# Program order for the evacuations of a seven-product matrix product, and four stores moved to one queue

## Chip, cores and metric

The kernel runs on one core of a Trainium2 chip. The metric is device microseconds of one execution, as the median of several runs. Beside the times there is one profiled execution, from which all rows below come.

## What is computed

Attention with a window of 128 and eight heads over 4 sequences of 576, then an MLP with ELU, then an MLP with leaky ReLU. The change lies in the second MLP and at the end of the first.

```python
x = np.ascontiguousarray(attn_out.transpose(0, 2, 1, 3)).reshape(B * S, H * D)   # 2304 x 512
# first MLP: d_ff 2048
h = x @ w_in
g = np.where(h > 0.0, h, 1.0 * (np.exp(np.minimum(h, 0.0)) - 1.0))
x = g @ w_out
# second MLP: d_ff 2048
h = x @ w_in
g = np.maximum(0.01 * h, h)
out = g @ w_out
```

## The kernel before

All matrix products run on operands that are split into a high and a low float32r part, so that one product is three matmuls (high by high, high by low, low by high; `split_mm`, L303). The split is always the same pair: a copy to float32r on ScalarE (the high part) and a subtraction on VectorE (the low part).

**First MLP.** Attention and the first MLP are interleaved over five blocks of tokens (`BLK1`). For each block, 16 chunks of the hidden width pass through `mlp1_h` (L559) and `mlp1_y` (L595). When the last chunk of a block is done, its result lies in four banks y0 to y3. They are copied to tiles ys, the even ones by ScalarE, the odd ones by VectorE (L619 to L622), and each is stored to x2T in DRAM (L625). The stores of the first three blocks are issued by SyncE, those of the last two by GpSimd (odd) and ScalarE (even).

**Second MLP, first product.** It works on three groups of 768 tokens (`GRP`) and, inside a group, on eight pairs of 128-wide chunks of the hidden width: 24 units. A unit multiplies a 2 x 2 block matrix of weights with a 2 x 2 block matrix of tokens by seven block products in place of eight (Strassen-Winograd). Each product is six matmuls of 128x128 by 128x384 (`product`, L820). The weight operands (tiles h1, h2 with their low parts) are sums of weight blocks, made earlier and kept in DRAM; they are loaded to a tile s for each pair (`s_load`, L742) and split for each unit (`split_w`, L748). The token operands (tiles x2) are sums of the four token blocks of a group. The group is loaded from x2T to a tile xr (`x2_load`, L765), and `x2_job` (L770) makes the seven operands in seven jobs, each a split and up to two subtractions.

`unit(u)` (L843) writes the work in this order: product 1 into bank x and copy s1 of it by ScalarE (L850); product 5 into bank z; product 4 of the unit before and its activation c21 (L856); product 6 into x and copy a by VectorE (L860); product 3 of the unit before, sum c12 on VectorE (L864) and its activation; product 2 into bank w, sum c11 (L869) and activation; product 7 into x, copy b by ScalarE (L873), sum c22 on VectorE (L875) and activation. Products 6, 7 and 4 go on adding to the bank that was copied just before, so each waits for that copy: 6 for s1, 7 for a, 4 (in the next unit) for b. In the profile the banks x, z, w are px, pz, pw. `g2_out` (L831) does the activation (L833, ScalarE) and the store to g2T in DRAM: by GpSimd for groups 0 and 1, by SyncE for group 2 (L836). The tiles a and c21 share three slots; a slot of c21 comes free when its store has landed.

**Second MLP, second product.** It reads g2T back and has the same seven products in another order (`second`, L936).

**What sets the order.** Matmuls are kept in the order of the program (`matmul`, L135). The other engines' instructions are placed by a scheduler, which takes them where it expects their operands and slots to be ready. Calls through the wrappers `act`, `dve`, `pool` are also kept in program order while `Ordered.on` is set (L126 to L131). Before the change the first product's evacuations and splits are called on `nc.scalar` and `nc.vector`, and so left to the scheduler. Each engine runs its instructions strictly in the order that results.

Of the kernel before, what the change touches and what calls it, by code (L numbers as in the profile page):

```python
# [10 lines left out]
F32 = mybir.dt.float32  # L11
# [4 lines left out]
AF = mybir.ActivationFunctionType  # L16
ALU = mybir.AluOpType
# [13 lines left out]
BLK1 = [(0, 512), (512, 256), (768, 512), (1280, 512), (1792, 512)]  # L31
# [67 lines left out]
def attention_elu_leaky_kernel(  # L99
# [13 lines left out]
    nc = tc.nc  # L113
# [481 lines left out]
    def mlp1_y(J, cs, gg):  # L595
        gh, gl = gg
        t0, n = BLK1[J]
        per = 512 // n
        if cs[0] == 0:
            Y[J] = [psp.tile([P, per, n], F32, tag=f"y{i}", name=f"y{i}") for i in range(NK // per)]  # L600
        for ci, i, m in [(ci, i, m) for ci in range(len(cs)) for i in range(3) for m in range(NK)]:
            woh, wol = weights(1, cs[ci], 1)
            w, g = ((woh, gh), (woh, gl), (wol, gh))[i]

            matmul(Y[J][m // per][:, m % per, :], w[:, m * P:(m + 1) * P], g[:, ci * n:ci * n + n],
                             start=cs[ci] == 0 and i == 0 and m % per == 0, stop=cs[ci] == NC - 1 and i == 2,
                             skip_group_check=True)
        if cs[-1] == NC - 1:
            if J == len(BLK1) - 1:

                all_ys = wp.tile([P, NK, n], F32, tag="w15", name="ys")
            for i, y in enumerate(Y.pop(J)):
                if J == len(BLK1) - 1:
                    ys = all_ys[:, i * per:i * per + per]
                elif J == len(BLK1) - 2 and i > 1:
                    ys = l2.tile([P, per, n], F32, tag="ex", name="ys", bufs=2)
                else:
                    ys = egp.tile([P, per, n], F32, tag="eg", name="ys")
                if i % 2:  # L619
                    nc.vector.tensor_copy(ys, y)  # L620
                else:
                    nc.scalar.copy(ys, y)  # L622

                q = nc.sync if J < len(BLK1) - 2 else nc.gpsimd if i % 2 else nc.scalar
                q.dma_start(out=x2T[:, i * per:i * per + per, t0:t0 + n], in_=ys)  # L625


# [142 lines left out]
    def x2_job(g, n):  # L770

        xr = Xr[g]

        def b(j, k):
            return xr[:, 2 * j:2 * j + 2, k * HALF:(k + 1) * HALF]

        def sub(o, x, y):
            nc.vector.tensor_tensor(o, x, y, op=ALU.subtract)

        def split(name, src):  # L780
            i = OPERANDS.index(name)
            home = OP_HOMES[g][i]
            if home == "x1":
                two = g, i // 3
                if two not in OP:
                    OP[two] = x1p.tile([P, 2, 2, 2, HALF], F32R, tag="x1", name="x2")
                t = OP[two][:, i % 3 % 2]
            else:
                t = (l2 if home[0] == "a" else wp).tile([P, 2, 2, HALF], F32R, tag=home, name="x2")
            nc.scalar.copy(t[:, 0], src)  # L790
            nc.vector.tensor_tensor(t[:, 1], src, t[:, 0].bitcast(F32), op=ALU.subtract)
            OP[g, name] = t[:, 0], t[:, 1]

        if n == 0:
            split("b11", b(0, 0))
            sub(b(0, 0), b(0, 1), b(0, 0))
            sub(b(0, 1), b(1, 1), b(0, 1))
        elif n == 1:
            split("t1", b(0, 0))
            sub(b(0, 0), b(1, 1), b(0, 0))  # L800
        elif n == 2:
            split("t2", b(0, 0))
            sub(b(0, 0), b(1, 0), b(0, 0))
        elif n == 3:
            split("b21", b(1, 0))
        elif n == 4:
            split("t3", b(0, 1))
        elif n == 5:
            split("t4", b(0, 0))
        elif n == 6:  # L810
            split("b22", b(1, 1))

    ps2, first, queue = {}, [], []

    def feed(n=1):
# [14 lines left out]

    def g2_out(u, c, half, tile_, src):  # L831
        g, p = divmod(u, NP2)
        nc.scalar.activation(tile_, src, AF.Prelu, alpha=0.01)  # L833
        t0 = g * GRP + half * HALF
        last = g == NG - 1
        store = (nc.sync if last else nc.gpsimd).dma_start(out=g2T[:, 2 * p + c, t0:t0 + HALF], in_=tile_)  # L836
        if last:
            tc.keep_in_program_order(store)
# [4 lines left out]
    def unit(u):  # L843

        if u < NU:
            x, z, w = (psp.tile([P, HALF], F32, tag=tg[u % 2], name=nm)
                       for tg, nm in ((("s0", "s1"), "px"), (("h", "c"), "pz"), (("y0", "y1"), "pw")))
            product(1, u, x, True)
            s1 = small(glp, "gh", "s1")
            nc.scalar.copy(s1, x)  # L850
            product(5, u, z, True)
        if u:
            x_, z_, a_ = ps2.pop(u - 1)
            product(4, u - 1, x_, False)
            c21 = small(glp, "gl", "c21")
            g2_out(u - 1, 1, 0, c21, x_)  # L856
        if u < NU:
            product(6, u, x, False)
            a = small(glp, "gl", "a")
            nc.vector.tensor_copy(a, x)  # L860
        if u:
            product(3, u - 1, z_, False)
            c12 = small(egp, "eg", "c12")
            nc.vector.tensor_tensor(c12, z_, a_, op=ALU.add)  # L864
            g2_out(u - 1, 0, 1, c12, c12)
        if u < NU:
            product(2, u, w, True)
            c11 = small(egp, "eg", "c11")
            nc.vector.tensor_tensor(c11, w, s1, op=ALU.add)  # L869
            g2_out(u, 0, 0, c11, c11)  # L870
            product(7, u, x, False)
            b = small(glp, "gh", "b")
            nc.scalar.copy(b, x)  # L873
            c22 = l2.tile([P, HALF], F32, tag="ex", name="c22", bufs=2)
            nc.vector.tensor_tensor(c22, z, b, op=ALU.add)  # L875
            g2_out(u, 1, 1, c22, c22)
            ps2[u] = x, z, a

# [32 lines left out]
    def prepare(n):  # L911

        g, at_ = divmod(n, len(SEQ))
        if g == NG:
            return
        m, q = SEQ[at_]
        cell = {r: RAW4[g, r][q] for r in ("b11", "b12", "b21", "b22") if len(RAW4.get((g, r), ())) > q}
        hi, lo = CELLS[n % 5]
        role = {1: "b11", 5: "b11", 6: "b11", 4: "b11", 7: "b12", 2: "b21", 3: "b22"}[m]
        split2(hi, lo, cell[role])  # L920
        D2[n] = hi, lo

        def sub(o, x, y):
            dve.tensor_tensor(cell[o], cell[x], cell[y], op=ALU.subtract)

        if m == 1:
            sub("b11", "b12", "b11")
        elif m == 5:
            sub("b11", "b22", "b11")
        elif m == 6:  # L930
            sub("b11", "b21", "b11")
            sub("b12", "b22", "b12")
# [81 lines left out]
    def raw_cells(role, home, tag, n):  # L1014
        cells = quarters(home.tile([P, 2 * n, HALF], F32, tag=tag, name="raw"), n)
        for cell in cells:
            raw_load(0, role, len(RAW4.get((0, role), ())), cell)

    for u in range(NU):
        g, p = divmod(u, NP2)  # L1020
        unit(u)
        if 0 < u < NU - 1:
            split_w(u + 1, 1)
        if u < NU - 1:
            split_w(u + 1, 2)
        if g == 0 and p < 5:
            s_load(p + 3)
        if g and p == 0:
            x2_job(g, 5)
            x2_job(g, 6)  # L1030
        if g + 1 < NG:
            if p == (g > 0):
                x2_load(g + 1)
            elif 4 <= p <= 6:
                x2_job(g + 1, p - 4)
            elif p == 7:
                x2_job(g + 1, 3)
                x2_job(g + 1, 4)
            continue
        if p == 1:  # L1040
            raw_cells("b11", l2, "xr", 4)
            xa = quarters(x1p.tile([P, 10, HALF], F32R, tag="x1", name="cells"), 5)
            CELLS += [(xa[0], xa[1]), (xa[2], xa[3])]
        elif p == 2:
            hl_load(1)
        elif p == 3:
            raw_cells("b12", wp, "w15", 2)
            raw_cells("b12", wrawp, "wraw", 2)
        elif p == 4:
            hl_load(5)  # L1050
        elif p == 5:
            prepare(0)
            hl_load(6)
        elif p == 6:
            prepare(1)
# [3 lines left out]
    xb = quarters(x1p.tile([P, 10, HALF], F32R, tag="x1", name="cells"), 5)  # L1059
    CELLS += [(xb[0], xb[1]), (xb[2], xb[3]), (xa[4], xb[4])]  # L1060
    prepare(2)
    unit(NU)
    raw_cells("b22", l2, "at0", 2)
    raw_cells("b21", l2, "at1", 2)
    for _ in range(2):
# [68 lines left out]
```

## Time and profile before

| | |
|---|---|
| median of 3 runs | 893.24 us (892.77 to 893.8) |
| profiled execution, its own time | 892.43 us |
| its span | 890.7 us |
| TensorE busy | 874.3 us, 98% |
| VectorE, ScalarE, GpSimd busy | 70%, 56%, 17% |
| mean granted clock of TensorE | 0.996 |

Times in the rows are microseconds from the start of the span. PE is TensorE's matmuls, PEld its weight loads, DVE is VectorE, ACT ScalarE, POOL GpSimd and SP SyncE; a q behind a name is the engine's sequencer, which issues DMAs. L127 and L136 are the lines of the wrappers, so that operations called through them are told apart by their tiles. The granted clock is 1.00 for 2.4 GHz and 0.50 for 1.2 GHz.

### The profile page before, as it was taken

How to read it: one execution, taken by the hardware profiler on the slowest of the kernel's cores; microseconds unless marked ns; L12 is line 12 of the kernel's file. 1: busy time of each engine (PE TensorE's matmuls, PEld its weight loads, DVE VectorE, ACT ScalarE, POOL GpSimd, SP SyncE). 2: the span in 40 equal slices, each digit the busy share in tenths (PEclk: the TensorE clock that was granted, in tenths of full speed). 3: DMA queues.
4: the chain of work that ended last, by engine and by line, in shares of the span. 5: the costliest groups of instructions: out<-in, count | busy, mean ns of one | idle time of the engine just before them, and what ended most of it. 6: DMA issues, size and time to landing. Idle time of an engine off the chain costs nothing. (4 is left out here: it accounts for less than half of the span.)

```text
span 890.7 us, 14687 instructions
## 1 busy us (share of the span) xinstructions
PE 874.3 (98%) x5077; PEld 770.7 (87%) x5077; DVE 621.9 (70%) x1330; ACT 499.5 (56%) x1067; POOL 155.4 (17%) x349
## 2 busy tenths in 40 slices
PE   8999999999999999999999989999999999999998
PEld 5578878998787787878888878999999999999998
DVE  6799866556776766677554786678577695875953
ACT  7888864445455555445443645677677544444442
POOL 5802222332213211121000001322310000000000
PEclk9999999999999999999999998999999999999999
DMA  8941323221745547353599999243239899437002
GB/s 327 347 177 61 120 74 107 59 71 49 261 154 202 191 160 271 132 220 146 180 344 367 312 308 395 108 158 133 110 110 312 331 358 372 162 100 233 23 1 71
DMA packets 94746, 169.66 MB, mean 190 GB/s; under 512 B 8144, under 2 KB 63696, under 8 KB 94672
## 3 DMA queue, kind: packets, MB, share of 16 engines
q1 hardware_dynamic: 89680, 154.04, 49.9%
q0 software_dynamic: 4416, 13.64, 4.1%
q10 hardware_dynamic: 576, 1.05, 0.3%
q8 instruction: 40, 0.66, 0.3%
q14 instruction: 34, 0.28, 0.1%
HBM read 106.82 MB, written 61.87 MB: 189 GB/s over the span
## 5 line engine op out<-in xcount | busy, mean ns | idle before, releaser
L136 PE MATMUL h_ps<-x,w 128*128 128x512 f32 (+1 forms) x960 | 215.0, 373 | 0.9 <-ACT x L127 0.5
L136 PEld LDWEIGHTS h_ps<-x,w 128*128 128x128 f32 x960 | 166.1, 188 | 38.8 <-ACT x L127 4.0
L136 PE MATMUL y<-gh,w 128*128 128x512 f32 (+1 forms) x640 | 157.2, 368 | 0.0
L136 PEld LDWEIGHTS y<-gh,w 128*128 128x128 f32 x640 | 113.8, 189 | 20.0
L880 ACT CAST cells<-raw 128x768 fp32r<-128x768 f32 x84 | 70.2, 837 | 86.8 <-PE px L136 46.3
L881 DVE TENSOR_TENSOR cells<-raw,cells 128x768 fp32r<-128x768 f32 x84 | 79.5, 956 | 41.9 <-ACT cells L880 41.4
L136 PE MATMUL px<-x,h 128*128 128x384 f32 x432 | 99.8, 338 | 5.3 <-ACT s L850 2.7
L136 PE MATMUL px<-cells,a 128*128 128x384 f32 x576 | 102.1, 334 | 0.3 <-ACT c L979 0.3
L136 PEld LDWEIGHTS px<-cells,a 128*128 128x128 f32 x576 | 100.0, 188 | 0.6 <-ACT c L979 0.6
L589 ACT CAST gh<-eg 128x512 fp32r<-128x512 f32 (+1 forms) x80 | 46.2, 577 | 82.0 <-DVE eg L588 81.7
L127 POOL TENSOR_SCALAR t<-t,stat 128x128 f32<-128x128 f32 (+3 forms) x160 | 71.7, 461 | 91.0 <-DVE stat L127 86.5
L127 ACT ACTIVATE t<-t,stat 128x128 f32<-128x128 f32 (+2 forms) x160 | 62.5, 393 | 43.6 <-DVE t L127 30.1
L136 PEld LDWEIGHTS px<-x,h 128*128 128x128 f32 x432 | 77.4, 189 | 6.8 <-ACT b L873 3.3
L127 POOL TENSOR_SCALAR_AFFINE_SELECT pt<-pt 128x256 f32<-128x256 f32 (+1 forms) x112 | 45.5, 415 | 213.9 <-ACT pt L489 210.3
L136 PE MATMUL y<-gl,w 128*128 128x512 f32 (+1 forms) x320 | 78.7, 368 | 0.0
L590 DVE TENSOR_TENSOR gl<-eg,gh 128x512 fp32r<-128x512 f32 (+1 forms) x80 | 51.1, 639 | 25.4 <-ACT gh L589 25.3
L136 PEld LDWEIGHTS y<-gl,w 128*128 128x128 f32 x320 | 56.9, 189 | 10.0
L762 ACT CAST h<-s 128x512 fp32r<-128x512 f32 (+1 forms) x72 | 49.4, 692 | 27.1 <-PE pz L136 25.6
L586 ACT ACTIVATE eg<-h_ps 128x512 f32<-128x512 f32 (+1 forms) x80 | 43.9, 548 | 35.6 <-PE h_ps L136 34.2
L127 DVE CUSTOM_DVE_ANT_0 t<-s_ps,bias 128x256 f32<-128x256 f32 (+4 forms) x160 | 51.6, 370 | 3.7 <-PE s_ps L136 2.9
L136 PE MATMUL pz<-x,h 128*128 128x384 f32 x240 | 54.1, 339 | 0.0
L588 DVE TENSOR_TENSOR eg<-h_ps,eg 128x512 f32<-128x512 f32 (+1 forms) x80 | 50.8, 636 | 2.0
(83 smaller groups left out, 1347.7 us busy)
## 6 DMA issues: line engine op xcount, KB each, us to landing
raw<-g2T SPq DMA_DIRECT2D x48, 384.0 KB, 4.8
wraw<-in_w_in SPq DMA_DIRECT2D x32, 512.0 KB, 5.1
wraw<-in_w_out SPq DMA_DIRECT2D x32, 512.0 KB, 4.9
hlT<-hl SPq DMA_DIRECT2D x16, 1024.0 KB, 5.9
a<-hlT SPq DMA_DIRECT2D x56, 256.0 KB, 5.2
g2T<-c POOLq DMA_DIRECT2D x64, 192.0 KB, 2.2
four<-s_out SPq DMA_DIRECT2D x16, 512.0 KB, 7.1
g2T<-c SPq DMA_DIRECT2D x32, 192.0 KB, 3.9
```

Source lines behind the costliest of these rows:

```text
L127: ins = f(*args, **kw)
L136: tc.keep_in_program_order(nc.tensor.matmul(*args, **kw))
L586: nc.scalar.activation(g[:, :m], ps, AF.Exp)
L588: nc.vector.tensor_tensor(g[:, :m], ps, g[:, :m], op=ALU.max)
L589: nc.scalar.copy(hi[:, :m], g[:, :m])
L590: nc.vector.tensor_tensor(lo[:, :m], g[:, :m], hi[:, :m].bitcast(F32), op=ALU.subtract)
L762: nc.scalar.copy(hi[:, a:b], s[:, a + o:b + o])
L880: nc.scalar.copy(hi, src)
L881: nc.vector.tensor_tensor(lo, src, hi.bitcast(F32), op=ALU.subtract)
```

## The change

The stores of the last block of the first MLP are all issued by GpSimd. In the first product of the second MLP the copies, sums and activations of `unit` and the splits and subtractions of `x2_job` are called through `act` and `dve`; `unit` and the jobs that follow units run with `Ordered.on`. (The jobs of group 0 run during the first MLP with it off.)

```diff
-                q = nc.sync if J < len(BLK1) - 2 else nc.gpsimd if i % 2 else nc.scalar
+                q = nc.sync if J < len(BLK1) - 2 else nc.gpsimd if i % 2 or J == len(BLK1) - 1 else nc.scalar
                 q.dma_start(out=x2T[:, i * per:i * per + per, t0:t0 + n], in_=ys)
...
         def sub(o, x, y):
-            nc.vector.tensor_tensor(o, x, y, op=ALU.subtract)
+            dve.tensor_tensor(o, x, y, op=ALU.subtract)
...
-            nc.scalar.copy(t[:, 0], src)
-            nc.vector.tensor_tensor(t[:, 1], src, t[:, 0].bitcast(F32), op=ALU.subtract)
+            act.copy(t[:, 0], src)
+            dve.tensor_tensor(t[:, 1], src, t[:, 0].bitcast(F32), op=ALU.subtract)
...
+    def ordered_job(g, *ns):
+        Ordered.on = True
+        for n in ns:
+            x2_job(g, n)
+        Ordered.on = False
...
-        nc.scalar.activation(tile_, src, AF.Prelu, alpha=0.01)
+        act.activation(tile_, src, AF.Prelu, alpha=0.01)
...
-            nc.scalar.copy(s1, x)
+            act.copy(s1, x)
...
-            nc.vector.tensor_copy(a, x)
+            dve.tensor_copy(a, x)
...
-            nc.vector.tensor_tensor(c12, z_, a_, op=ALU.add)
+            dve.tensor_tensor(c12, z_, a_, op=ALU.add)
...
-            nc.vector.tensor_tensor(c11, w, s1, op=ALU.add)
+            dve.tensor_tensor(c11, w, s1, op=ALU.add)
...
-            nc.scalar.copy(b, x)
+            act.copy(b, x)
...
-            nc.vector.tensor_tensor(c22, z, b, op=ALU.add)
+            dve.tensor_tensor(c22, z, b, op=ALU.add)
...
     for u in range(NU):
         g, p = divmod(u, NP2)
+        Ordered.on = True
         unit(u)
+        Ordered.on = False
...
         if g and p == 0:
-            x2_job(g, 5)
-            x2_job(g, 6)
+            ordered_job(g, 5, 6)
         if g + 1 < NG:
             if p == (g > 0):
                 x2_load(g + 1)
             elif 4 <= p <= 6:
-                x2_job(g + 1, p - 4)
+                ordered_job(g + 1, p - 4)
             elif p == 7:
-                x2_job(g + 1, 3)
-                x2_job(g + 1, 4)
+                ordered_job(g + 1, 3, 4)
...
+    Ordered.on = True
     unit(NU)
+    Ordered.on = False
```

In the rows of the order below, a number behind a tile is the tile's own, and the brackets name the engines and DMA lanes that the instruction waits for.

The first place is ScalarE from the end of the first MLP into unit 1 of the first product, before the change. h_5778 is a weight operand of unit 2, x_6028 the first token operand of group 1; c_5687 and c_5699 are c11 and c22 of unit 0, c_5735 and c_5752 its c21 and c12, and c_5762 is c11 of unit 1.

```order
L622 COPY ys<-y_5043 128x512 [waits PE_49]
L622 COPY ys<-y_5045 128x512
L625 DMA x2T<-ys 128x512 [waits Activation_49] x2
L850 COPY s_5665<-px 128x384 [waits PE_49]
...
L850 COPY s_5721<-px 128x384 [waits PE_49]
L833 ACTIVATE c_5735<-px 128x384 [waits PE_49]
L790 CAST x_6028<-xr 128x768 [waits DMAHW3_49]
L762 CAST h_5784<-s 128x512 [waits PE_49]
L833 ACTIVATE c_5752<-c_5752 128x384 [waits DVE_49]
L762 CAST h_5857<-s 128x512 [waits DMAHW1_49,PE_49]
L833 ACTIVATE c_5762<-c_5762 128x384 [waits DVE_49]
L873 COPY b<-px 128x384 [waits PE_49,Activation_49]
```

The same place on ScalarE after the change.

```order
L622 COPY ys<-y_5043 128x512 [waits PE_49]
L622 COPY ys<-y_5045 128x512
L127 COPY s_5665<-px 128x384 [waits PE_49]
...
L127 COPY s_5721<-px 128x384 [waits PE_49]
L127 ACTIVATE c_5735<-px 128x384 [waits PE_49]
L762 CAST h_5784<-s 128x512 [waits PE_49]
L127 ACTIVATE c_5752<-c_5752 128x384 [waits DVE_49]
L127 ACTIVATE c_5762<-c_5762 128x384 [waits DVE_49]
L127 COPY b<-px 128x384 [waits PE_49,Activation_49]
L762 CAST h_5857<-s 128x512 [waits DMAHW7_49]
```

The two DMA issues behind the ys copies are gone. The token operand x_6028, which waits for a load, and the weight cast h_5857, which waits for another, no longer stand ahead of copy b of unit 1; h_5857 stands behind it, and x_6028 between c21 and c12 of the unit before, in unit 4.

The second place is GpSimd's queue from the stores of the last two blocks on, before the change.

```order
L625 DMA x2T<-ys 128x512 [waits DVE_49] x2
L836 DMA g2T<-c_5687 128x384 [waits Activation_49]
L836 DMA g2T<-c_5699 128x384 [waits Activation_49]
L836 DMA g2T<-c_5735 128x384 [waits Activation_49]
L836 DMA g2T<-c_5752 128x384 [waits Activation_49]
```

And after it.

```order
L625 DMA x2T<-ys 128x512 [waits Activation_49]
L625 DMA x2T<-ys 128x512 [waits DVE_49]
L625 DMA x2T<-ys 128x512 [waits Activation_49]
L625 DMA x2T<-ys 128x512 [waits DVE_49]
L842 DMA g2T<-c_5687 128x384 [waits Activation_49]
L842 DMA g2T<-c_5699 128x384 [waits Activation_49]
L842 DMA g2T<-c_5735 128x384 [waits DMASW0_49,Activation_49]
L842 DMA g2T<-c_5752 128x384 [waits DMASW1_49,Activation_49]
```

Four stores of 256 KB in place of two now stand ahead of the first stores of the first product.

The third place is VectorE in units 1 and 2 after the change; the first row is copy a of unit 1, c_5774 is c22 of unit 1, and the last row is copy a of unit 2.

```order
L127 COPY a<-px 128x384 [waits PE_49]
L127 TENSOR_TENSOR c_5752<-pz,a 128x384 [waits DVE_49,PE_49]
L763 TENSOR_TENSOR h_5784<-s,h_5784 128x512 [waits Activation_49]
L127 TENSOR_TENSOR c_5762<-pw,s_5721 128x384 [waits PE_49]
L127 TENSOR_TENSOR c_5774<-pz,b 128x384 [waits DMASW1_49,Activation_49]
L763 TENSOR_TENSOR l_5858<-s,h_5857 128x512 [waits DMAHW7_49,PE_49,Activation_49]
L763 TENSOR_TENSOR l_5858<-s,h_5857 128x768 [waits DMAHW4_49,Activation_49]
L127 COPY a<-px 128x384 [waits DMASW0_49,PE_49]
```

Copy a of unit 2 waits for lane DMASW0, the lane of the store of c_5735, which is c21 of unit 0. Before the change two subtractions and a split of group 1's token operands stood between these rows; they now come in units 4 and 5.

## Rows read from the trace of the kernel before

**Rows 1.** The page, busy us (share of the span) and instructions of each engine.
```profile
PE 874.3 (98%) x5077; PEld 770.7 (87%) x5077; DVE 621.9 (70%) x1330; ACT 499.5 (56%) x1067; POOL 155.4 (17%) x349
```

**Rows 2.** Busy us by stretches, PE, PEld, DVE, ACT, POOL, clock, DMA share, GB/s.
```profile
520.00:540.00 20.00, 17.26 (x81) 15.74 (x80) 12.96 (x18) 10.13 (x17) 2.16 (x4) 0.91 0.97 331
540.00:560.00 20.00, 17.97 (x95) 17.65 (x94) 13.90 (x21) 11.53 (x22) 4.61 (x9) 0.91 0.87 346
600.00:700.00 100.00, 100.00 (x577) 99.57 (x576) 72.39 (x112) 68.98 (x134) 17.11 (x32) 1.00 0.53 190
720.00:740.00 20.00, 20.00 (x117) 20.00 (x116) 17.20 (x21) 8.70 (x11) 0.00 (x0) 1.00 1.02 371
```

**Rows 3.** Line of time, TensorE, 526 to 556: start, us, operation [idle before <- releaser].
```profile
531.93 0.61 PE L136 MATMUL px<-x,h 128*128 128x384 f32 x2 [2.74 <-ACT s L850]
...
536.75 0.52 PE L136 MATMUL px<-x,h 128*128 128x384 f32 x2
...
544.04 0.51 PE L136 MATMUL px<-x,h 128*128 128x384 f32 x2
...
548.32 1.77 PE L136 MATMUL px<-x,h 128*128 128x384 f32 x8 [2.03 <-ACT b L873]
...
555.19 0.51 PE L136 MATMUL px<-x,h 128*128 128x384 f32 x2
```

**Rows 4.** Busy us by stretches, the granted clock third from the end.
```profile
532.70:536.00 3.30, 3.30 (x12) 3.30 (x11) 0.88 (x2) 0.00 (x0) 0.00 (x0) 0.50 0.99 299
...
549.80:553.10 3.30, 3.30 (x12) 3.30 (x12) 3.15 (x5) 1.14 (x3) 1.08 (x2) 0.50 1.03 408
...
225.50:229.00 3.50, 3.50 (x20) 2.67 (x18) 2.98 (x13) 1.19 (x7) 1.57 (x4) 1.00 0.97 370
```

**Rows 5.** Line of time, ScalarE and its sequencer, 529 to 549.
```profile
529.14 1.06 ACT L622 COPY ys<-y 128x512 f32<-128x512 f32 x2
529.75 1.61 ACTq L625 DMA_DIRECT2D x2T<-ys  x2
531.40 0.48 ACT L850 COPY s<-px 128x384 f32<-128x384 f32 x1 [1.19 <-issue]
...
540.08 0.49 ACT L833 ACTIVATE c<-px 128x384 f32<-128x384 f32 x1 [0.61 <-PE px L136]
545.05 0.84 ACT L790 CAST x<-xr 128x768 fp32r<-128x768 f32 x1 [4.47 <-DMA xr<-x2T]
...
547.80 0.46 ACT L873 COPY b<-px 128x384 f32<-128x384 f32 x1
```

**Rows 6.** Line of time, GpSimd, 530 to 542.
```profile
530.95 1.14 POOL L625 DMA_DIRECT2D x2T<-ys  x2 [82.89 <-DVE ys L620]
...
540.87 0.54 POOL L836 DMA_DIRECT2D g2T<-c  x1 [0.93 <-ACT c L833]
```

**Rows 7.** Line of time, TensorE, 215 to 230, in the first MLP.
```profile
224.01 1.09 PE L136 MATMUL av_ps<-pt,vr 128*64 128x128 f32 x16 [1.47 <-DVE eg L588]
```

**Rows 8.** DMA issues, 529 to 534.5: count, KB each, us to landing.
```profile
xr<-x2T SPq DMA_DIRECT2D x1, 1536.0 KB, 13.8
```

**Rows 9.** The page, costliest groups: busy us, mean ns of one.
```profile
L881 DVE TENSOR_TENSOR cells<-raw,cells 128x768 fp32r<-128x768 f32 x84 | 79.5, 956 | 41.9 <-ACT cells L880 41.4
```

**Rows 10.** Line of time of SyncE's sequencer; DMA issues around 534.
```profile
532.39 2.82 SPq L745 DMA_DIRECT2D s<-s_in  x2
...
s<-s_in SPq DMA_DIRECT2D x1, 512.0 KB, 13.7
```

**Rows 11.** DMA, 540.5 to 546.5: queue, packets, MB, share; an issue, us to landing.
```profile
q0 software_dynamic: 193, 0.59, 24.3%
...
g2T<-c POOLq DMA_DIRECT2D x1, 192.0 KB, 5.4
```

**Rows 12.** DMA queues, 534.5 to 537.5: q10 is ScalarE's, q0 GpSimd's.
```profile
q10 hardware_dynamic: 280, 0.52, 45.2%
...
q0 software_dynamic: 63, 0.25, 20.0%
```

## Prediction

> **What bounds the kernel now.** I read the page's busy times first: TensorE is busy 98% of the span [rows 1], so only TensorE's own time counts, and a change of order on the other engines can give back no more than what TensorE loses to waits and to a lower clock. Next the busy times by stretches: everywhere in the second MLP TensorE's column equals the stretch (100.00 of 100 at 600 to 700, all of 20 at 720 to 740 in the second product), except in 520 to 540 and 540 to 560, where 17.26 and 17.97 of 20 are busy and the granted clock is 0.91 [rows 2]. So the place to look is the start of the first product. TensorE's own line of time there shows two holes [rows 3]: it stands still for 2.74 us before it starts again at 531.93, and for 2.03 us before 548.32; the brackets name what ended the wait. The first hole is ended by the ScalarE copy s of bank px, the second by the copy b of the same kind. After each hole the granted clock is at 0.50, the lower of its two levels (1.2 against 2.4 GHz), for the 3.3 us that I cut out behind it [rows 4]. Last, ScalarE's line of time says why the copies were late [rows 5].
>
> **Terms used.** A unit has seven products of six matmuls. At the full clock one unit takes 544.04 - 536.75 = 7.29 us [rows 3], so a product takes 1.04 us. In a unit: products 1 and 5, then 4 of the unit before, 6, 3 of the unit before, 2, 7. Copy s must end before product 6 starts, which is two products after product 1; copy b of a unit before the next unit's product 4, two products after that unit's product 7.
>
> **The stores of the last block (ScalarE's half).** After its two ys copies ScalarE issues two stores, 1.61 us in all, and only then starts copy s, at 531.40 [rows 5]. The second issue could not start before the second ys copy was done (529.14 + 1.06 = 530.20). With the issues on GpSimd's queue copy s follows the ys copies directly: the copies of a pair overlap a little (two of about 0.58 in 1.06), so it starts at about 530.13 in place of 531.40, 1.27 us earlier; TensorE then starts at 530.66 in place of 531.93. Everything ahead of it on ScalarE stays as it was, so a hole of 2.74 - 1.27 = 1.47 us remains. **Gain 1.27.** GpSimd was idle; it gets two issues more. Its two stores of before take 1.14 us from 530.95 [rows 6], so four go from about 530.0 to 532.7, and the next thing on it (the store of c11 of unit 0) is due only after 534. The issue is hidden there; what the transfers may cost is rival B and C.
>
> **The clock after the first hole.** From product 6 of unit 0 to product 1 of unit 1 TensorE took 536.75 - 531.93 = 4.82 us for three products [rows 3]; at the full clock they take 3.12. Whether the clock falls after a hole of 1.47 us the two holes here (2.74 and 2.03) do not tell. The nearest row is the wait of 1.47 us at 224.01 [rows 7]: the stretch behind it stands at 1.00 [rows 4]. I take that row, since it has the same length: **gain 1.70**, with 0 as the other end.
>
> **Evacuations and token operands in program order.** On ScalarE the copy x (first half of the token operand b11 of group 1) stood before copy b of unit 1, and it waited 4.47 us for the load of xr [rows 5], which took 13.8 us from its issue [rows 8]. Behind it stood two weight casts, two activations, and b, which came at 547.80 while its bank was ready at about 544.1. In the new order that copy x stands in unit 4, some 15 us after the load has landed at 545.05, and no instruction ahead of b of unit 1 waits for a transfer. Product 4 then follows product 5 without a hole: at 544.04 + 2.08 = 546.12 in place of 548.32, **gain 2.20**; and products 4, 6, 3, 2, 7 take 5.20 in place of 555.19 - 548.32 = 6.87 [rows 3] at the full clock, **gain 1.67**. VectorE loses the same wait. The eleven subtractions of a group's token operands go mostly two at a time between c11 and c22 of units 4 to 8 (and 12 to 16) in place of scattered. One of this shape takes 0.96 us [rows 9], so c22 comes up to 1.9 us later; but its bank is only needed by product 3 of the next unit, four products (4.2 us) after product 7. In 600 to 700, where this work lies, VectorE was busy 72% and ScalarE 69% [rows 2], so I cost the move at 0 there; if it did not fit, a copy a would come late, at most by one such subtraction in each of ten units.
>
> **Casts that may be late next.** The weight cast for unit 4 stands ahead of copy s of unit 3, and waits for a load s. That load is the second of two issues between 532.39 and 535.21 and took 13.7 us [rows 10], so it landed by 548.9 at the latest. By the new times the cast is wanted behind copy b of unit 2, at 533.78 + 2 x 7.29 + 0.6 = 549.0 (533.78 is the new start of product 1 of unit 1), and copy s could be 1 us later without harm. The casts for units 3 and 5 have more room. I cost them at 0, and at 1 us at the upper end.
>
> **Sum.** 1.27 + 1.70 + 2.20 + 1.67 = 6.84 us, from the profiled execution's 892.43 us (span 890.7) to 885.6. The median of the runs shown is 893.24, so the forecast for the median is 893.24 - 6.84 = **886.4 us**; alone its range is 885.4 to 887.4. Behind the units the rest moves up as it is: loads and stores of the second product are issued in the order of the units, on the same queue.
>
> **Rivals.**
> A. *The clock falls after the first hole all the same.* For it: 1.47 us is not far from 2.03, after which it fell. Against it: the hole of 1.47 us without a fall. It would leave out the 1.70: 888.1. The Trainium skill (TensorE: Matmul & The Clock Gate, What's actually happening) says that the activity is watched in free-running windows, so that one kernel can meet them at another phase from run to run; by that rule a borderline hole would go either way, and the sum would be 886.4 in some runs and 888.1 in others. No run here shows such a change.
>
> B. *Stores land late and a slot is waited for.* All four stores of the last block now go ahead of the stores of c11, c22, c21 of unit 0 on GpSimd's one queue. The copy a of unit 2 takes the slot of c21 of unit 0. By the new times c21 is issued at about 537.9 (3.0 earlier than the 540.87 of [rows 6]), and with the 5.4 us of [rows 11] it lands at 543.3; copy a is wanted when product 6 of unit 2 ends, at 533.78 + 7.29 + 4.16 = 545.2, and delays product 7, two products later, only if it starts after about 546.8. Bounds: ScalarE's queue moved 0.52 MB in 3 us, 173 GB/s [rows 12]; at that rate and from 535 on, where ScalarE's stores began to move, the four stores (1.05 MB) are through at 541.1 and three small ones (0.59 MB) at 544.5. GpSimd's queue in 540.5 to 546.5 moved 0.59 MB in 6 us, 98 GB/s [rows 11]; at 98 for the small ones alone they are through at 547.1, 0.3 us too late. I take a delay of 0.3 to 1.5 us here, up to 3 with a fall of the clock: 887 to 889.5. Against it: the 98 GB/s were three small stores that came one after another, not a full queue.
>
> C. *Slower than before by the same queue.* If GpSimd's queue moves only 80 GB/s from 535 on, 1.64 MB take 20.5 us, c21 lands at 555.5, 8.7 us too late, and the clock falls once more (1.7): 886.4 + 10.4 = 896.8. The point from which it decides is 98 GB/s over the whole of it: landing at 551.7, 4.9 late, plus 1.7, which eats the whole gain. For it: the DMA engines are at their full share there, and ScalarE's queue no longer carries a part. Against it: 173 GB/s in the same crowd. The Trainium skill (DMA: Bandwidth & Descriptors, Queues, rings and completion order) has each DMA engine go round between the queues that have work. By that rule GpSimd's queue gets about half beside SyncE's, C cannot come, and the time is that of the forecast. The quarter that [rows 11] shows does not prove it, so C keeps a chance.
>
> D. *The gain does not reach the end.* In 720 to 740 the DMA engines are at 1.02 of their share [rows 2]; if the loads of the second product were held by something that does not move with the units, TensorE would wait there for what it gained, and the time would be 893. Against it: their issues follow the units, and TensorE is busy 20.00 of 20 in that very stretch [rows 2].
>
> **Chances.** Forecast 0.64, A 0.14, B 0.08, D 0.07, C 0.07. A change under 0.2% (1.8 us) cannot be told from none here. Forecast, A and B are faster by more than that: 0.86. D is the same: 0.07. C is slower: 0.07. The range takes in the forecast's own range, A and B with a fall of the clock, and leaves out C and D; A and B together stand at its upper end: 885.0 to 890.6.
>
> **What would show it.** Right: ScalarE goes from the ys copies to copy s without an issue between; one hole of about 1.5 us before product 6 of unit 0 and the clock at 1.00 behind it; no hole before product 4 of unit 1; units at 7.29 us from there on; copy x of group 1 in unit 4 with no wait for xr. Wrong: a granted clock of 0.5 after 530 (A); a TensorE hole before product 7 of unit 2 that is ended by a VectorE copy a, which itself was ended by a store of c (B, C); TensorE waits behind 704 that were not there (D).

## The result and the profile after

The changed kernel took **886.34 us** (median of 5 runs, 884.8 to 889.25) against 893.8 us for the kernel before (5 runs, 892.77 to 895.13): a ratio of 0.992, 95% interval 0.9897 to 0.9942, so 5.2 to 9.2 us less. 886.4 was forecast. The execution that was profiled is the longest of the five: 889.25 us, span 887.5.

The page of the changed kernel, engines' busy times (before: [rows 1]):

```profile
PE 872.8 (98%) x5077; PEld 769.5 (87%) x5077; DVE 623.0 (70%) x1330; ACT 498.7 (56%) x1067; POOL 157.1 (18%) x351
```

Only POOL has two instructions more, the two stores. The work is the same, so the gain is in waits and in the clock. Busy times of the changed kernel by stretches, columns as in [rows 2]; the last two stretches are 3.2 us that begin 1.5 us after TensorE's restart behind the first hole, and the place where [rows 4] has the clock behind the second:

```profile
520.00:540.00 20.00, 16.98 (x78) 15.26 (x77) 13.52 (x20) 9.95 (x16) 2.69 (x5) 0.91 0.92 299
540.00:560.00 20.00, 20.00 (x117) 20.00 (x116) 12.23 (x20) 11.64 (x24) 5.77 (x11) 1.00 1.03 412
...
720.00:740.00 20.00, 20.00 (x118) 20.00 (x117) 15.84 (x19) 7.59 (x10) 0.00 (x0) 1.00 1.05 387
534.90:538.10 3.20, 3.20 (x11) 3.20 (x11) 0.95 (x2) 0.52 (x1) 0.56 (x2) 0.50 0.99 259
549.80:553.10 3.30, 3.30 (x21) 3.30 (x21) 2.28 (x4) 1.46 (x3) 0.97 (x2) 1.00 1.04 416
```

540 to 560 was 17.97 busy at a clock of 0.91 and is now full at 1.00. In 520 to 540 nothing is better: 16.98 busy, 0.91. TensorE's line of time shows the same at single matmuls (before: [rows 3]):

```profile
533.38 0.62 PE L136 MATMUL px<-x,h 128*128 128x384 f32 x2 [3.02 <-ACT s L127]
...
538.14 0.56 PE L136 MATMUL px<-x,h 128*128 128x384 f32 x2
...
545.47 0.51 PE L136 MATMUL px<-x,h 128*128 128x384 f32 x2
...
547.55 1.55 PE L136 MATMUL px<-x,h 128*128 128x384 f32 x8
...
552.75 0.51 PE L136 MATMUL px<-x,h 128*128 128x384 f32 x2
```

The second hole is gone: product 4 of unit 1 starts at 547.55, which is 545.47 + 2.08, two products behind product 1 of unit 2, and no bracket stands there. The first hole is 3.02 us, longer than the 2.74 of before, and 4.76 us pass from its end to product 1 of unit 1 (before 4.82; 3.12 would be the full clock). ScalarE's line of time of the changed kernel (before: [rows 5]):

```profile
529.01 1.05 ACT L299 CAST hl<-four 128x1024 fp32r<-128x1024 f32 x1 [2.87 <-DMA four<-s_out]
529.97 0.82 ACT L127 CAST x<-xr 128x768 fp32r<-128x768 f32 x1
531.36 0.62 ACT L762 CAST h<-s 128x512 fp32r<-128x512 f32 x1 [0.56 <-DVE hl L300]
531.88 1.07 ACT L622 COPY ys<-y 128x512 f32<-128x512 f32 x2
532.84 0.49 ACT L127 COPY s<-px 128x384 f32<-128x384 f32 x1
...
545.44 0.53 ACT L127 ACTIVATE c<-c 128x384 f32<-128x384 f32 x1 [0.73 <-DVE c L127]
545.87 0.46 ACT L127 COPY b<-px 128x384 f32<-128x384 f32 x1
...
565.95 0.84 ACT L127 CAST x<-xr 128x768 fp32r<-128x768 f32 x1
```

VectorE's has copy a of unit 2, which follows its bank and not a store:

```profile
549.83 0.56 DVE L127 COPY a<-px 128x384 f32<-128x384 f32 x1 [0.45 <-PE px L136]
```

Copy s follows the ys copies without an issue between, as forecast, and copy b of unit 1 comes at 545.87 without copy x ahead of it; copy x stands at 565.95, without a wait. What is new to the argument is the first of ScalarE's rows. It is the cast of the last tile `four` (the load of an operand of the second product), five instructions ahead of copy s; it waits for its load, and all behind it wait with it. The weight cast two rows further waits 0.56 us more, for VectorE's subtraction of the same tile. The cast's row of the kernel before, which the prediction does not use:

```profile
526.28 1.05 ACT L299 CAST hl<-four 128x1024 fp32r<-128x1024 f32 x1 [1.80 <-DMA four<-s_out]
```

The DMA issues say in part why it starts later after (issue to landing, first the changed kernel, then the one before):

```profile
four<-s_out SPq DMA_DIRECT2D x1, 512.0 KB, 8.1
```

```profile
four<-s_out SPq DMA_DIRECT2D x1, 512.0 KB, 7.1
```

SyncE's sequencer has the rest, in the same order:

```profile
520.90 0.66 SPq L291 DMA_DIRECT2D four<-s_out  x1
```

```profile
519.18 0.66 SPq L291 DMA_DIRECT2D four<-s_out  x1
```

The load takes 1.0 us longer, and against the end of product 5 of unit 0 (530.36 after, 529.19 before) it is issued 0.55 us later: 9.46 us ahead of it in place of 10.01. In both profiles its issue comes 0.64 us behind that of the store of the split before, which goes out when VectorE has done the subtraction of that split; so a late landing one tile earlier moves this issue too.

**The first hole in one sum.** From the start of this cast to TensorE's restart it is 533.38 - 529.01 = 4.37 us after, and 531.93 - 526.28 = 5.65 us before. The difference, 1.28, is the two issues. But the cast starts 1.35 us before product 5 of unit 0 ends (533.38 - 3.02 = 530.36) after, and 2.91 us before its end (531.93 - 2.74 = 529.19) in the profile of before. So the hole is 4.37 - 1.35 = 3.02 after, against 5.65 - 2.91 = 2.74.

**Where the profiled execution's time went.** At the end of product 5 of unit 0 it was 1.17 us later than the one before (530.36 - 529.19), a difference out of the first MLP. The first hole took 0.28 more, the three products behind it 0.06 less. Then the two units with the place of the second hole: from product 1 of unit 1 to product 1 of unit 3 it is 552.75 - 538.14 = 14.61 us after, twice 7.3, and 555.19 - 536.75 = 18.44 before [rows 3]: **3.83 less**, where the prediction has 2.20 + 1.67 = 3.87. That leaves 2.44 us won at this point; the span won 3.2, and the 0.8 in the 330 us behind it I did not follow.

### The profile page after: what moved, and what is told of

The parts are those of the page before. It is cut to its first block, busy times and chain, and to the rows that moved or that the text cites. A ratio compares the mean times of both kernels' runs of the same rounds, so it can differ in the third digit from the quotient of the medians.

```text
span 887.5 us, 14689 instructions
## 1 busy us (share of the span) xinstructions
PE 872.8 (98%) x5077; PEld 769.5 (87%) x5077; DVE 623.0 (70%) x1330; ACT 498.7 (56%) x1067; POOL 157.1 (18%) x351
```

## Experiments

The theory after these rows: the moved copy x gives the second hole with its clock; the stores give 1.27 us, and the clock behind the first hole only where the load of the last `four` lands early. Rivals: the order of the units themselves is what counts; or the first hole is the stores' and should have closed. The first four kernels ran on one chip (before there: 893.98, 17 runs, 891.18 to 895.53).

**Stores alone.** The kernel before with the edit of line 624, nothing else.

> Only the stores of the last block go to GpSimd; evacuations and operands are placed as before. My theory (two separate holes): the first hole shrinks by 1.27 us, and where the clock then stays up, 1.70 us more; the second hole and its clock loss (2.20 + 1.67) stay. Time 1.3 to 3.0 us under the kernel before, about 891. Rival (the first hole is set by the late load of four that ScalarE's last cast hl waits for, not by the two DMA issues): the hole stays at 2.5 to 3 us and the time is within 0.7 us of the kernel before.

892.91 us (11 runs), ratio 0.9991 (0.9981 to 1.0001): 1.1 us less by the medians. Both holes are there:

```profile
PE px L136 <- ACT s L850: 3.0, 1, 3.0
PE px L136 <- ACT b L873: 2.9, 2, 2.3
```

This is TensorE's list of waits from 525 to 885 (us in total, times, longest); a second wait for b, 0.6 us in the last unit, is in the 2.9. ScalarE's line of time, then TensorE's:

```profile
527.87 1.05 ACT L299 CAST hl<-four 128x1024 fp32r<-128x1024 f32 x1 [2.74 <-DMA four<-s_out]
```

```profile
532.24 0.93 PE L136 MATMUL px<-x,h 128*128 128x384 f32 x2 [3.02 <-ACT s L850]
```

The hole did not shrink; it stands at 3.02, as the rival in the expectation has it. Yet from cast to restart it is 4.37 us, as in the changed kernel: the issues are gone, and the cast comes later. The gain in time fits the 1.27, but its interval (-0.1 to 1.7 us) takes in no gain too; it is too small for 1.27 and the 1.70 of a clock that stays up.

**Order alone.** The changed kernel with line 624 as it was.

> Only the program order of evacuations and token operands; the stores stay on ScalarE and GpSimd. My theory: the second hole and its clock loss go (2.20 + 1.67 = 3.9 us), the first hole stays at 2.7 us or more, with the clock at 0.50 behind it. Time about 3.9 us under the kernel before, about 889.9. Rival (the gain needs both parts, because the late store issues also hold the second hole's load): under 2 us.

888.98 us (6 runs), ratio 0.9943 (0.9924 to 0.9961), 3.5 to 6.8 us less. The second hole is gone; the first is 3.56 us, and the 5.8 us that I cut out behind it have a granted clock of 0.50. ScalarE's line of time with the order alone:

```profile
526.53 1.05 ACT L299 CAST hl<-four 128x1024 fp32r<-128x1024 f32 x1 [2.63 <-DMA four<-s_out]
...
530.01 1.59 ACTq L625 DMA_DIRECT2D x2T<-ys  x2
531.65 0.48 ACT L127 COPY s<-px 128x384 f32<-128x384 f32 x1 [1.18 <-issue]
```

TensorE's, in the same kernel:

```profile
532.18 1.01 PE L136 MATMUL px<-x,h 128*128 128x384 f32 x2 [3.56 <-ACT s L127]
```

And the stretch behind it, columns as in [rows 2]:

```profile
532.20:538.00 5.80, 5.80 (x18) 5.80 (x19) 1.12 (x2) 0.52 (x1) 0.25 (x2) 0.50 1.01 328
```

With the issues back, cast to restart is 532.18 - 526.53 = 5.65 us, as before.

**The change once more.**

> The changed kernel once more, for a second profile and five more times. If the first hole's length changes from run to run with the landing of the last load of four, runs with a mean clock of 1.000 lie 2 to 4 us under runs with 0.997 or 0.998, and this profile has another hole than 3.02 us. Rival (the hole is always 3 us and the spread comes from elsewhere): a hole of 3.0 us and a clock of 0.50 behind it again.

887.43 us (6 runs, 884.08 to 890.91), ratio 0.9922 (0.9901 to 0.9943). The profiled execution has a hole of 3.55 us; ScalarE's line of time, then TensorE's:

```profile
529.86 1.05 ACT L299 CAST hl<-four 128x1024 fp32r<-128x1024 f32 x1 [3.28 <-DMA four<-s_out]
```

```profile
534.22 0.62 PE L136 MATMUL px<-x,h 128*128 128x384 f32 x2 [3.55 <-ACT s L127]
```

Cast to restart is again 4.36; this load took 8.5 us. Over the two groups of runs of the changed kernel the mean granted clock of the span goes with the time: the five executions of 0.999 or 1.000 took 884.1 to 886.3 us, the six of 0.997 or 0.998 took 887.2 to 890.9.

**The late cast taken away.** The last `four` is cast in unit 1, behind copy s, together with the weight split that stood in unit 0.

```
-        four_split(c)
+        if c < NC - 1:
+            four_split(c)
...
             act.copy(s1, x)
+            if u == 1:
+                four_split(NC - 1)
+                split_w(1, 2)
             product(5, u, z, True)
...
-        if u < NU - 1:
+        if 0 < u < NU - 1:
             split_w(u + 1, 2)
```

> The change, and the last split of four (cast hl on ScalarE, subtraction on VectorE) with the weight split that waits for its slot moved from the end of the first MLP into unit 1, behind copy s. If the load of four is what keeps ScalarE from copy s of unit 0, the first hole goes as a whole: no hole over 0.5 us at the start of the first product, no fall of the clock, and 883 to 884.5 us, 1.5 to 3 us under the changed kernel. If copy s is late for another reason (the ys copies, VectorE), a hole of over 1 us stays and the time is that of the changed kernel. If the moved work is too much for unit 1, a hole comes in unit 1 or 2 instead.

The split's instructions are also written through the ordered engines there. 884.6 us (4 runs, 884.06 to 886.79), ratio 0.9897 (0.9884 to 0.9911), 2.8 us less than the change on the same chip, by medians whose intervals just overlap. The five executions of the changed kernel at 0.999 or 1.000 are as fast as these, 884.1 to 886.3; by these runs the move takes away the slower ones. ScalarE's line of time, then the stretch that holds the place of the first hole:

```profile
528.82 1.08 ACT L622 COPY ys<-y 128x512 f32<-128x512 f32 x2 [1.88 <-PE y L136]
529.88 0.48 ACT L127 COPY s<-px 128x384 f32<-128x384 f32 x1
```

```profile
520.00:540.00 20.00, 20.00 (x105) 18.44 (x103) 14.19 (x20) 11.48 (x20) 3.23 (x6) 1.00 1.02 360
```

Now ScalarE waits for TensorE (1.88 us for bank y) and not the other way round; the stretch is full at 1.00. This settles the first hole: what held copy s was the split of the last `four` and the weight split that waits for it. The two were moved together, so what each held up is not told apart. What is left are small waits, in TensorE's list from 525 to 885:

```profile
PE px L136 <- ACT c L988: 1.3, 1, 1.3
PE px L136 <- ACT b L127: 0.6, 1, 0.6
PE px L136 <- DVE a L127: 0.5, 1, 0.5
```

Next came four kernels on another chip (before there: 894.09, 17 runs, 891.1 to 896.1).

**Which part of the order counts.** First only the units in program order, with the token jobs where the scheduler had put them; then only the token jobs, with the units left to the scheduler.

In ordered_job (line 814):

```
-        Ordered.on = True
+        Ordered.on = False
```

> The change with the token operands of groups 1 and 2 left to the scheduler; only the units' evacuations are in program order. The copy x that waits for xr then stands ahead of copy b of unit 1 again. If the place of that one copy is the whole of the second hole, the hole of 2 us or more and the clock at 0.50 are back, the gain of e2 is lost, and the time is that of e1, about 1 us under the kernel before. Rival (the order of the evacuations themselves matters): a hole under 1 us and about 3 us or more gained.

Around the units:

```
-        Ordered.on = True
         unit(u)
-        Ordered.on = False
...
-    Ordered.on = True
     unit(NU)
-    Ordered.on = False
```

> The change with the units' evacuations left to the scheduler and only the token operands of groups 1 and 2 in program order. If the place of copy x is all that counts, this has the time of the changed kernel, 6 to 7 us under the kernel before, with no second hole. Rival: evacuations stand out of order and small holes come in the units; 1 us or more slower than the changed kernel.

Units only: 892.42 us (12 runs), ratio 0.9985 (0.9973 to 0.9998). Jobs only: 887.57 us (6 runs), ratio 0.9933 (0.9908 to 0.9957). ScalarE's line of time with the units only:

```profile
545.94 0.83 ACT L127 CAST x<-xr 128x768 fp32r<-128x768 f32 x1 [3.57 <-DMA xr<-x2T]
...
547.10 0.46 ACT L127 COPY b<-px 128x384 f32<-128x384 f32 x1
```

Copy x is back ahead of copy b and waits for the same load; TensorE waits 2.2 us for b and the clock falls a second time (0.59 in 548.5 to 552.0). At the first hole, ScalarE and then TensorE:

```profile
526.86 1.05 ACT L299 CAST hl<-four 128x1024 fp32r<-128x1024 f32 x1 [2.84 <-DMA four<-s_out]
```

```profile
531.22 1.01 PE L136 MATMUL px<-x,h 128*128 128x384 f32 x2 [2.65 <-ACT s L127]
```

With the jobs only, ScalarE's order is that of the change, and TensorE's list of waits has only one long one, for s:

```profile
PE px L136 <- ACT s L127: 2.2, 1, 2.2
PE px L136 <- ACT b L127: 0.6, 1, 0.6
```

Its rows at the first hole:

```profile
526.64 1.05 ACT L299 CAST hl<-four 128x1024 fp32r<-128x1024 f32 x1 [2.46 <-DMA four<-s_out]
```

```profile
531.00 0.79 PE L136 MATMUL px<-x,h 128*128 128x384 f32 x2 [2.23 <-ACT s L127]
```

So the place of the token jobs makes the gain of the order; the order of the units' own evacuations adds nothing to be seen.

**Twice as many stores on GpSimd's queue.** The kernel without the late cast, with four stores more of the last block to a scratch array, also on GpSimd.

```
+            if J == len(BLK1) - 1:
+                nc.gpsimd.dma_start(out=x2X[...], in_=ys)
```

> The kernel of e4 with the four stores of the last block doubled on GpSimd's queue (the second four go to a scratch tensor that nothing reads). This measures how much room the slot of c21 has. If the queue moves 173 GB/s, 1.05 MB more take 6 us; in the changed kernel's profile the store of c21 of unit 0 landed at 548.1 and copy a of unit 2 was due at 549.8 and harmless until 551.4, so a hole of 2 to 4 us before product 7 of unit 2 that is ended by VectorE's copy a, with the clock at 0.50 behind it: 3 to 6 us slower than e4. Rival (room of over 6 us: the stores share the engines and land hardly later): no hole there, within 1 us of e4.

885.31 us (4 runs), ratio 0.9914 (0.9887 to 0.9942). Rival B's wait comes, and costs little; VectorE's line of time, then TensorE's, whose first row is product 3 of unit 1; it starts when product 6 of unit 2 has filled copy a's bank:

```profile
546.48 0.56 DVE L127 COPY a<-px 128x384 f32<-128x384 f32 x1 [2.78 <-DMA g2T<-c]
```

```profile
544.32 1.20 PE L136 MATMUL pz<-x,h 128*128 128x384 f32 x6
...
547.09 0.62 PE L136 MATMUL px<-x,h 128*128 128x384 f32 x2 [0.53 <-DVE a L127]
```

VectorE stands 2.78 us until the store of c21 has landed, and copy a of unit 2 starts 2.2 us after its bank is full; the two products in between cover most of that, and TensorE stands 0.53. My expectation of a hole of 2 to 4 us was wrong. It had counted those two products; its error was the landing, which it moved by 6 us (1.05 MB at 173 GB/s). Against the bank the store of c21 lands 0.2 us early in the kernel without the late cast (540.26 + 5.6, the bank at 546.03) and 2.1 late here (539.81 + 6.6), so the four stores moved it by 2.3. Rival C falls by the queues' rows in 535 to 541 (packets, MB, share of the DMA engines' time):

```profile
q0 software_dynamic: 400, 1.31, 53.9%
q1 hardware_dynamic: 398, 1.18, 48.7%
```

GpSimd's queue moved 1.31 MB in 6 us, 218 GB/s, where C needed 98 or less. The Trainium skill (DMA: Bandwidth & Descriptors, Queues, rings and completion order) has each DMA engine go round between the queues that have work; these shares, about half each, agree. In the changed kernel itself the queue's stores move from about 538 on, and its row for 538 to 542 has 0.98 MB in 4 us, 245 GB/s:

```profile
q0 software_dynamic: 289, 0.98, 60.6%
```

**The stores back on ScalarE, without the late cast.**

```
-                q = nc.sync if J < len(BLK1) - 2 else nc.gpsimd if i % 2 or J == len(BLK1) - 1 else nc.scalar
+                q = nc.sync if J < len(BLK1) - 2 else nc.gpsimd if i % 2 else nc.scalar
```

> The kernel of e4 with the stores of the last block on ScalarE and GpSimd as before the change. With the load of four out of the way, the two issues on ScalarE are all that is left ahead of copy s. If they are worth what the prediction says, a hole of 0.5 to 1.5 us comes before product 6 of unit 0 and the time is 0.5 to 3 us above e4 (the more where the clock falls). Rival (they cost nothing once ScalarE is early): no hole, and the time of e4.

885.42 us (6 runs, 884.8 to 885.94), ratio 0.9906 (0.9889 to 0.9924), against 884.6 with the stores on GpSimd, on another chip, with overlapping intervals. TensorE's wait for s is there, 0.3 us, less than the 0.5 to 1.5 expected, and the clock stays at 1.00:

```profile
PE px L136 <- ACT s L127: 0.3, 1, 0.3
```

With copy s no longer late by the cast, the issues of 1.2 us nearly fit: by these rows the first half of the change is worth its 1.27 only behind a late cast.

**A better version.** On a third chip (before there: 892.08, 11 runs, 890.68 to 896.3), the kernel without the late cast, with the weight split behind copy a in place of copy s, and two slots of their own for c21 of the second product, whose copy had waited 0.87 us for a store. The weight split's instructions are written through the ordered engines here too.

```
-            if u == 1:
-                four_split(NC - 1)
-                split_w(1, 2)
+            if u == 1:
+                four_split(NC - 1)
...
             dve.tensor_copy(a, x)
+            if u == 1:
+                split_w(1, 2)
...
-            c21 = small(glp, "gl", "c21")
+            c21 = l2.tile([P, HALF], F32, tag="ex", name="c21", bufs=2)
```

> The kernel of e4 with its two remaining small holes taken on: the weight split of unit 1 behind copy a of unit 1 on VectorE (hole of 0.5 us before product 7 of unit 1), and tile c21 of the second product in slots of its own (hole of 0.3 to 1.3 us at its first product 4, where ScalarE waited for an earlier store to out). If both holes are real time, 0.8 to 1.8 us under e4 and 883 to 884 us. Rival (the end of the kernel is set by transfers there, so that the wait only moves): within 0.4 us of e4.

> The kernel of e4 once more, on the chip of e9 and with the same runs of the kernel before: 884 to 885.5 us, ratio 0.988 to 0.991, and again no hole over 0.6 us at the start of the first product and no fall of the clock.

882.9 us (5 runs, 882.04 to 884.24), ratio 0.9895 (0.9873 to 0.9917); the kernel it is built on took 884.64 us there (6 runs), ratio 0.9916 (0.9897 to 0.9935). The only wait of TensorE left between 525 and 885 is

```profile
PE px L136 <- ACT b L127: 0.6, 1, 0.6
```

It is the fastest of all by its median, though its interval and that of the kernel without the late cast overlap. What each of its two parts is worth is open: the wait for c that the slots take away was 1.3 us in one profile of the kernel without the late cast and 0.4 in the other. Against the changed kernel it was not run on one chip.

## Why the prediction was right, and where it was not

- **What bounds the kernel: right.** The work is unchanged, and what the profiled execution won, all but 0.8 us, lies in the second of the two stretches of [rows 2] that were not full; the first came only with the late cast taken away.
- **The second hole, 2.20 + 1.67: right in mechanism and size.** Product 4 stands two products behind product 1, the clock is 1.00, and copy x, in unit 4, waits for nothing. The profiled pair gives 3.83 us for 3.87, and the order alone gave 3.5 to 6.8 us over all runs. Of the parts of the order, only the token jobs bring it.
- **The stores, 1.27: right as a term.** Cast to restart is 4.36 to 4.37 us without the issues in five profiles and 5.65 with them in both. As time it is not shown: the stores alone gave 1.1 us, not clear of none.
- **The failed step** is "Everything ahead of it on ScalarE stays as it was, so a hole of 2.74 - 1.27 = 1.47 us remains." It does not stay: it hangs on a load whose issue and landing move from run to run. The table has all seven profiles that hold the late cast there; times in us. The load's lead is from its issue to the end of product 5 of unit 0; the cast's lead is that minus the landing (but for rounding), and the hole is cast to restart minus the cast's lead.

| kernel | load's lead | `four`, us to landing | cast's lead | cast to restart | hole |
|---|---|---|---|---|---|
| before | 10.01 | 7.1 | 2.91 | 5.65 | 2.74 |
| order alone | 9.97 | 7.9 | 2.09 | 5.65 | 3.56 |
| jobs only | 9.84 | 7.7 | 2.13 | 4.36 | 2.23 |
| units only | 9.79 | 8.1 | 1.71 | 4.36 | 2.65 |
| change | 9.46 | 8.1 | 1.35 | 4.37 | 3.02 |
| stores alone | 9.33 | 8.0 | 1.35 | 4.37 | 3.02 |
| change again | 9.34 | 8.5 | 0.81 | 4.36 | 3.55 |

The one profile that I had is the one with the earliest cast of the seven, and its 892.43 us are on the short side of the runs of before (median 893.98 of 17 on the first chip of the experiments). With its 2.91 the changed kernel's hole would be 1.46, as forecast.
- **The clock after the first hole, 1.70: not shown as a sure term.** In both profiles of the change it fell, behind holes of 3.02 and 3.55. The mean clock of the span is 1.000 in all five profiles without a fall and 0.995 to 0.998 in all seven with one or two, so I take it that the five executions of the change at 0.999 or 1.000 had none; the six others can have had one. No trace of the five exists, so how long their hole was stays open; a shorter hole after an earlier landing would explain them. The Trainium skill (TensorE: Matmul & The Clock Gate, What's actually happening) speaks of free-running windows, by which one hole could go either way; no run here tells that from a shorter hole.
- **Why 886.4 still came out: in part luck.** It lies between two kinds of executions. The six have a median of 888.3 us, near the sum without its 1.70 (888.1, the price of rival A). The five have one of 884.8, about 9 us under the medians of before, 2 us more than the whole sum. The two are 3.5 us apart, twice the 1.64 (4.76 - 3.12) that the fall took in the profile, so the fall alone does not part them. The order's 5.0 by medians, 1.1 more than its term, may be in it, but its interval holds the term as well; this is not settled. Nor is it that the clock tells all: with the jobs only, one execution at a mean clock of 1.000 took 884.3 us and three took 887.3 to 889.5.
- **Rivals.** A is what the profiled executions show, by a longer hole than A had in mind. B's slot was no wait. Copy a of unit 2 follows its bank, and even twice the stores cost 0.53 us of TensorE. C and D did not come: the queue moved 245 GB/s where C needed 98 or less, and 720 to 740 is full as before.
- **Casts late next: 0, right.** No wait of that kind is in TensorE's list.

## What to carry to other kernels

Before you subtract from a hole, follow the waiting engine's chain back past the edited instruction to the last one that waited for something else: here that was the cast of a load, five instructions earlier, and the landing set the hole, so the remedy was to move the cast and what hangs on it. An instruction that waits for a transfer does not belong ahead of an evacuation that TensorE needs; of the whole reordering, the place of the token jobs was all the gain that can be seen. Size a term that hangs on a landing by a span of landings, not by one profile.

## What the runs showed of the hardware

- The same load of 512 KB, with the same work beside it, took 7.1 to 8.5 us to land over seven profiles, and TensorE's restart followed it. In the five profiles with its cast moved it took 6.6 to 8.4, and TensorE's hole there was 0.32 us at most.
- GpSimd's queue reached 218 and 245 GB/s beside SyncE's when it had stores waiting, against 98 GB/s in [rows 11], where it was fed one small store at a time; a low rate in a trace need not be a limit.
- In all twelve profiles the clock fell after every hole of 2.03 us and more (2.03 to 3.56), and not after 1.47 us [rows 7] or 1.27 us (the wait for c in the kernel without the late cast). That the length decides is not shown: one execution of the order alone had a mean clock of 1.000, and by its 5.65 and the longest lead of the table its hole is estimated at 2.74 us or more; it has no trace.
